# An S5 scan and a dilated local attention on one core: a memset moved to GpSimd, V's weight loads put on the Activation queue, and a new written-out order

## The chip, the cores and the metric

The kernel runs on one core of one Trainium2 chip. The metric is device time in microseconds of one execution. Before the change the median of three runs is 137.35 us (137.34 to 138.31).

## The reference, cut to what matters

Two independent layers read two inputs of 2048 rows and 448 columns in bf16, and their outputs stand side by side in the 896 columns of the result.

```python
# A: a diagonal complex state space layer
Bu = einsum("bld,pd->blp", x, B_bar)
h  = Lam_bar * h + Bu[:, t]                 # over 2048 steps
y  = 2 * einsum("blp,dp->bld", hseq, C).real + x * Dskip
# B: attention over 8 keys, 2 rows apart, 16 heads of 28
q, k, v = split(x @ wqkv)
attn = softmax(q . k[t - 2w] * scale, masked where t < 2w)
out  = (sum_w attn * v[t - 2w]) @ wo
```

## The kernel before, in words

The sequence of B is split into two halves of 1024 rows (index `b`). Weights and `x` are laid out so that the contraction runs over 128 rows: channel blocks are kept once for even and once for odd positions, so the weight matrix for Q and K (`wqk`, part of the tile `rb`) is loaded once and then copied to the other half of the partitions by `shift` (copies at L205 on DVE or L201 on ACT). The copies come in three column blocks: "a" (columns 0 to 127, loaded by L359 on the ACT queue), "b" (128 to 255) and "c" (256 to 447), both loaded by L359 on the SP queue. Each block has a copy of 64x6 and one of 64x8 rows; the second also needs the last 64 weight rows, loaded by L361 on the ACT queue. V's weights are a tile of their own (`wv`, `load_v`, lines L336 to L340 of `wload`): the even copy of 336 KB and 56 KB, and the odd copy of the same sizes, four transfers.

`x` for B arrives by transposing transfers: the first half in four pieces (`half(h, m)`, L348: `h` the quarter of the sequence, `m` the pair of positions), the second half in four pieces (`load(1, j)`, L352). For A, `x` arrives in 16 such transfers (L865, tile `xaT_sb`), and the matrices B by L845 and L846.

Projections of Q and K go first: for the first half `first(kt, h)` (L492) makes a pair of column blocks for 512 rows, with `h = 0` needing the first two pieces of `x` and `h = 1` the other two; block "c" and the leftover columns, and the whole second half, are made by `proj` (L451). Products of Q with shifted K are formed on DVE (L557, 18 instructions of 128x2048 or 128x4096), summed per head on PE with 32-column weights (L570), then softmax (L597, L606, L616 on ACT; L591, L625 on DVE). V's projection (L670) is spread to neighbours by transfers on SP (L696), DVE multiplies and adds (L724 to L741), transfers transpose the result (L768) and PE applies `wo` (L787, L794).

A's scan runs for seven groups `m` of 64 complex states: input projection (L1132), powers of Lambda as small matrices (`pw`, built by L1081 on DVE or as ten scaled copies on ACT), a tree of carries (L1149 to L1228) in which PE and ACT alternate, and the output product (L1316) with the skip term (L1335 on PE, or L1302 on DVE and L1328 on ACT).

The memsets and masks of `consts` and `consts2` stand ahead of everything else in the program: DVE clears tiles, GpSimd runs `affine_select` on them. In `consts2`, DVE clears the upper half of `Zhi` (L255) after GpSimd's second `affine_select` on it (L253).

All other work is cut into units, and each unit is added to a `Planner` with its engines, cost, latency and priority. The planner's result is written out: the list `ORDER` gives the units in program order (a number from 1000 up means the second of the unit's engines) and `BANKS` the PSUM banks. At build time `run` walks `ORDER`; costs and latencies no longer have any effect then. So each engine and each transfer queue executes its instructions in the order of that list, and waits by semaphores.

Transfers of the SP and ACT queues share eight semaphores (DMAHW0 to DMAHW7), handed out in turn in program order over both queues. A transfer waits, before its issue, for the landing of the transfer that had its semaphore before it, unless that is known to be done.

Of the kernel before, what the change touches and what calls it, by code (L numbers as in the profile page):

```python
# [9 lines left out]
ACT = mybir.ActivationFunctionType  # L10
# [6 lines left out]
D = 448  # L17
T = 16
# [11 lines left out]
JB = 8  # L30
SL = HALO + JB
NX = 7
KPAD = 16
# [41 lines left out]
]  # L75
BANKS = [
    0, 0, 2, 3, 5, 0, 2, 4, 6, 0, 2, 4, 6, 0, 6, 4, 0, 6, 4, 6, 0, 2, 4, 6, 7, 2, 0, 6, 7, 0, 7, 2, 0, 1, 2, 4,
    5, 2, 4, 5, 7, 2, 5, 2, 5, 3, 0, 2, 0, 5, 4, 7, 5, 0, 3, 2, 5, 0, 5, 0, 1, 6, 4, 6, 4, 6, 2, 0, 2, 0, 6, 4,
    2, 0, 2, 4, 6, 2,
# [112 lines left out]
class Ctx:  # L192
# [43 lines left out]
    def consts2(self):  # L236
        nc, pool, G, V = self.nc, self.pool, self.nc.gpsimd, self.nc.vector
# [17 lines left out]
        V.memset(Zh[0:64, :], 0.0)  # L255
# [56 lines left out]
class PartB:  # L312
# [9 lines left out]
    def loads(self):  # L322
# [24 lines left out]
        def half(h, m):  # L347
            nc.sync.dma_start(xh[:, 14 * m:14 * m + 14, 64 * h:64 * h + 64],  # L348
                              bass.AP(x.tensor, x.offset + 64 * h * JB * D + 4 * m * D, [[JB * D, 64], [1, 4 * D]]), transpose=True)
# [7 lines left out]
        def cols(eng, c0, c1):  # L357
            for a in range(2):
                eng.dma_start(w4[:, 0:3, a, c0:c1], src[:, :, a, c0:c1])  # L359
# [3 lines left out]
        self.u_w["a", 0] = P.add("ACTQ", 0.0, lambda: None, lat=5.6)  # L363
        self.u_wr = P.add("ACTQ", 0.0, lambda: None, lat=6.2)
        self.u_xh = {}
        for h in range(2):
            for m in range(2):
                self.u_xh[h, m] = P.add("SP", 1.33, lambda h=h, m=m: half(h, m), [self.u0], -9, lat=3.6 if h + m == 0 else 3.4, dma=1.04)
            c0, c1 = ((NCH, 2 * NCH), (2 * NCH, D))[h]
            self.u_w["bc"[h], 0] = P.add("SP", 0.95, lambda c0=c0, c1=c1: cols(nc.sync, c0, c1), [self.u0], -9, lat=3.4, dma=(0.9, 1.3)[h])  # L370
# [20 lines left out]
    def load_v(self, deps):  # L391
        def go():
            self.wload(self.nc.sync, 2 * D, 0)
            self.wload(self.nc.sync, 2 * D, 1)
        self.u_w[2] = self.plan.add("SP", 2.3, go, deps, 0.5, lat=1.6, dma=3.6)
# [30 lines left out]
    def prep(self, u_warm):  # L426
        nc, P, cx = self.nc, self.plan, self.cx
# [97 lines left out]
        for b in range(2):  # L525
            for n, (kind, kt) in enumerate((("K", 0), ("Q", 0), ("K", 1), ("Q", 1), ("K", 2), ("Q", 2), ("M", 3))):
                if b or kt > 1:
                    proj(b, kind, kt, -8 + b * 4 + 0.1 * n)

            def dup(b=b):  # L530
                t0, t1 = b * HB, (b + 1) * HB
                nc.sync.dma_start(self.k3[hi, KPAD + JB + t0:KPAD + JB + t1], self.k3[lo, KPAD + t0:KPAD + t1])
                nc.sync.dma_start(self.q3[hi, t0:t1], self.q3[lo, t0:t1])
            self.u_k[b, 3] = self.u_q[b, 3] = [P.add("SP", 1.0, dup, self.u_k[b, 3] + self.u_q[b, 3], -7, lat=1.5, dma=1.2)]
# [287 lines left out]
class PartA:  # L822
# [27 lines left out]
    def load_x(self, deps):  # L850
# [23 lines left out]
        for j in (0, 4, 8, 12, 2, 6, 10, 14, 1, 5, 9, 13, 3, 7, 11, 15):  # L874
            self.u_x[j] = P.add("SP", 1.36 if j < T - 1 else 1.9, lambda j=j: load(j), deps if j < T - 1 else [u0], 0.6, lat=1.6, dma=0.48)
# [22 lines left out]
    def setup(self):  # L898
# [132 lines left out]
        a4 = P.add("DVE", 1.9, u4, [a3], -5)  # L1031
# [443 lines left out]
```

## Time and profile before

| what | value |
|---|---|
| median of 3 runs | 137.35 us |
| the profiled execution's own time | 137.41 us |
| its span, first to last instruction | 135.7 us |
| outside the span | 1.7 us |
| PE, DVE, ACT, POOL busy | 126.7, 113.8, 99.1, 10.3 us |
| granted TensorE clock | 1.00 throughout |
| transfers | 20.25 MB, mean 149 GB/s |

PE is the tensor engine's matmuls and PEld its weight loads, DVE the vector engine, ACT the scalar engine, POOL GpSimd, SP the engine that issues most transfers; a q behind a name means its queue or sequencer. A row of the timeline gives the start in us from the span's start, the duration, the engine and line, what is written and read, the number of instructions merged into the row, and in brackets the idle time of the engine before it with what ended that. The chain of waits has start, duration and what ran. In a table by windows each engine has its busy time and number of instructions, then the granted clock, the mean busy share of the 16 DMA engines and the GB/s. The view of one source line ends with the time from a transfer's issue to its landing. In the DMA view q1 is the SP queue and q10 the ACT queue, with packets, MB and share of 16 engines. Busy PE is not PE at its peak: a 128x512 matmul is shown with some 380 ns, while the next one starts 216 ns later.

### The profile page before, as it was taken

To read this page: it belongs to the slowest core of one execution; us is meant where nothing else is said; L and a number is where in the kernel's file an instruction comes from. 1 tells how busy PE (TensorE), PEld (TensorE's weight loads), DVE (VectorE), ACT (ScalarE), POOL (GpSimd) and SP (SyncE) were. 2 spreads that over 40 slices of the span, in tenths; PEclk is the share of its full clock that TensorE was granted. 3 is DMA by queue.
4 is the path that set the end of the run, shared out by engine and by line. 5 is a ranking of instruction groups with operands and counts; after the bars stand their busy time and mean duration, and the time that the engine had idled before them with its cause. 6 is when DMAs were issued, how large, how long until landed. Compare 5 with 4: busy or idle time off the path is not lost.

```text
span 135.7 us, 2467 instructions
## 1 busy us (share of the span) xinstructions
PE 126.7 (93%) x921; PEld 63.5 (47%) x921; DVE 113.8 (84%) x133; ACT 99.1 (73%) x170; POOL 10.3 (8%) x27
## 2 busy tenths in 40 slices
PE   6859999999999689999999999999899999999990
PEld 2447543344446243565444455444556554455440
DVE  5069999999999996799999999999999999990100
ACT  3018999769797535798879997988889993527741
POOL 6934060000000000000000000000000000000000
PEclk9999999999999999999999999999999999999999
DMA  4999899589446586924669999261810394128432
GB/s 102 206 208 180 146 234 186 115 197 132 77 75 131 122 232 187 235 69 101 178 169 145 225 238 233 78 175 28 236 39 0 78 279 153 68 96 214 169 135 101
DMA packets 47759, 20.25 MB, mean 149 GB/s; under 512 B 38774, under 2 KB 46346, under 8 KB 47748
## 3 DMA queue, kind: packets, MB, share of 16 engines
q1 hardware_dynamic: 46676, 19.77, 62.8%
q10 hardware_dynamic: 880, 0.31, 1.1%
q8 instruction: 7, 0.11, 0.4%
q0 software_dynamic: 192, 0.03, 0.1%
q14 instruction: 4, 0.03, 0.1%
HBM read 5.18 MB, written 4.19 MB: 69 GB/s over the span
## 4 chain that ended last, share of the span: by engine, by line
PE 86%; ACT 4%; POOL 4%; issue 3%; DVE 1%; POOLq 0%; DVEq 0%; ACTq 0%
PE banks L1316 16%; PE banks L1132 15%; PE banks L451 12%; PE banks L670 8%; PE banks L787 7%; PE banks L570 6%; PE banks L492 5%; PE banks L1176 4%; PE banks L794 2%; PE banks L1149 2%; POOL prm L836 2%; PE banks L1189 1%; PE banks L1335 1%; PE banks L1056 1%; PE banks L1228 1%
## 5 line engine op out<-in xcount | busy, mean ns | idle before, releaser
L557 DVE TENSOR_TENSOR prods<-qk 128x4096 bf16<-128x4096 bf16 (+1 forms) x18 | 31.8, 1809 | 0.0
L1132 PE MATMUL banks<-xaT_sb,Bcat 128*128 128x512 bf16 (+1 forms) x112 | 27.0, 383 | 1.5 <-issue 1.5
L201 ACT CAST ra<-banks 128x896 bf16<-128x896 f32 (+2 forms) x24 | 18.5, 777 | 12.6 <-PE banks L1316 5.7
L201 ACT CAST qk<-banks 128x512 bf16<-128x512 f32 (+3 forms) x20 | 16.8, 844 | 2.4 <-PE banks L451 1.3
L730 DVE TENSOR_TENSOR prods<-prods 128x7168 bf16<-128x7168 bf16 x4 | 15.6, 3889 | 0.1
L724 DVE TENSOR_TENSOR prods<-ra 128x7168 bf16<-128x7168 bf16 x4 | 15.5, 3882 | 0.0
L724 DVE TENSOR_TENSOR prods<-ra,qk 128x7168 bf16<-128x7168 bf16 x4 | 15.4, 3883 | 0.0
L1132 PEld LDWEIGHTS <-Bcat 128*128 128x128 bf16 (+1 forms) x112 | 8.8, 99 | 12.9 <-issue 6.9
L1316 PE MATMUL banks<-Ccat,h 128*128 128x448 bf16 x64 | 14.7, 353 | 0.0
L451 PE MATMUL banks<-rb 128*128 128x512 bf16 (+1 forms) x64 | 13.9, 379 | 0.0
L670 PE MATMUL banks<-wv,rb 128*128 128x448 bf16 (+1 forms) x64 | 13.0, 354 | 0.0
L1171 ACT CAST pbuf<-banks 128x64 bf16<-128x64 f32 (+1 forms) x42 | 9.6, 233 | 3.4 <-PE banks L1176 2.2
L1316 PE MATMUL banks<-Ccat,qk 128*128 128x448 bf16 x48 | 12.0, 353 | 0.0
L787 PE MATMUL banks<-wo_p,rb 128*128 128x448 bf16 x48 | 11.1, 356 | 0.0
L1176 PE MATMUL banks<-pbuf,pw 128*128 128x64 bf16 x77 | 9.8, 235 | 0.6 <-ACT pbuf L1171 0.5
L492 PE MATMUL banks<-rb 128*128 128x256 bf16 (+2 forms) x76 | 7.3, 256 | 2.0 <-DVE rb L205 1.5
L203 ACT ACTIVATE qk<-banks 128x512 bf16<-128x512 f32 (+2 forms) x10 | 8.4, 848 | 0.8 <-PE banks L451 0.8
L1176 PEld LDWEIGHTS <-pw 128*128 128x128 bf16 x77 | 6.2, 105 | 5.5 <-issue 1.6
L1081 DVE TENSOR_TENSOR pw<-Dm,spair 128x640 bf16<-128x640 bf16 (+1 forms) x14 | 8.5, 649 | 0.0
L1316 PEld LDWEIGHTS <-h 128*128 128x128 bf16 x64 | 5.9, 98 | 5.3 <-issue 0.6
L451 PEld LDWEIGHTS <-rb 128*128 128x128 bf16 (+1 forms) x64 | 5.1, 97 | 6.7 <-issue 1.7
L670 PEld LDWEIGHTS <-rb 128*128 128x128 bf16 (+1 forms) x64 | 4.9, 98 | 6.2 <-issue 3.0
(144 smaller groups left out, 187.5 us busy)
## 6 DMA issues: line engine op xcount, KB each, us to landing
out_dram<-ra SPq DMA_DIRECT2D x12, 224.0 KB, 2.6
xaT_sb<-in_A_x_dram SPq DMA_DIRECT2D x2, 448.0 KB
out_dram<-ra SPq DMA_DIRECT2D x8, 112.0 KB, 1.7
ra<-ra SPq DMA_DIRECT2D x2, 392.0 KB, 3.8
qk<-qk SPq DMA_DIRECT2D x2, 392.0 KB, 3.8
wv<-in_B_wqkv_dram SPq DMA_DIRECT2D x2, 336.0 KB, 3.9
ra<-ra SPq DMA_DIRECT2D x1, 588.0 KB, 5.6
qk<-qk SPq DMA_DIRECT2D x1, 588.0 KB, 4.7
```

The lines of the kernel that those rows point to most:

```text
L201: nc.scalar.copy(out, in_)
L451: nc.tensor.matmul(out(e)[:, j0:j1], lhsT=w, rhs=self.xB[rows, b, j0:j1, c, :], start=e not in begun, stop=True, skip_group_check=True)
L492: nc.tensor.matmul(box["ps"][:, e, k, 64 * j0:64 * j1], lhsT=self.wqk[rows, c, D * k + NCH * kt:D * k + NCH * kt + NCH], rhs=self.xB[rows, ...
L557: V.tensor_tensor(p[:, :, a:a + n], q[:, t0 + a:t0 + a + n].unsqueeze(1).to_broadcast([NCH, 4, n]), bass.AP(k.tensor, k.offset, [k.ap[0], ...
L670: nc.tensor.matmul(box["ps"][:, e, 0:D], lhsT=self.xB[rows, b, jj, c, :], rhs=self.wv[rows, c, :], start=e not in begun, stop=True, skip_g ...
L724: V.tensor_tensor(out.rearrange("p (u i d h) -> p u i d h", u=4, i=4, d=DH), self.attn[b][:, r].rearrange("p (x u i) h -> p x u i h", x=2, ...
L730: V.tensor_tensor(T1, T1, T2, op=ALU.add)
L787: nc.tensor.matmul(ps, lhsT=o[:, kt + x, :], rhs=self.wo_p[:, (KT + 1) * x + kt, :], start=(kt == 0), stop=False, skip_group_check=True)
L1132: mt(ps(i), lhsT=lhsT, rhs=rhs, start=i not in begun, stop=True, **kw)
L1171: nc.scalar.copy(pb[:, dst, PAD:PAD + NCH // d], tot(a, d))
L1176: mt(tot(out, 2), lhsT=L(T * unit * k), rhs=pb[:, src, PAD - sh:PAD - sh + NCH // 2], start=False, stop=True, **kw)
L1316: nc.tensor.matmul(ps, lhsT=self.h[m][:, i, g * NCH:(g + 1) * NCH], rhs=self.Ccat[:, m, :], start=False, stop=(m == NM - 1), skip_group_ch ...
```

## The change

- In `consts2` the memset of `Zhi`'s upper half is on GpSimd, not DVE.
- `load_v` and the row copies `dup` (L532, L533) may be issued by SP or ACT. In the new list V's weights are on ACT (unit 134 is `1134`); both row copies are on SP, as before.
- Landing latencies and some costs given to the planner are changed, among them 2.5 us instead of 1.6 for A's `x`.
- `ORDER` and `BANKS` are new lists. Among the units that can go either way, two of the first-column `pw` builds (276 and 375) and one weight copy (17) are now on ACT, and two output evictions (590 and 595) on DVE.

```diff
 ORDER = [
-    3, 0, 1, 23, 4, 15, 2, 5, 6, 7, 9, 39, 41, 43, 16, 47, 8, 44, 45, 24, 46, 18, 25, 27, 40, 42, 59, 57, 17,
...
+    0, 1, 23, 3, 2, 5, 6, 15, 7, 8, 9, 10, 4, 41, 39, 16, 40, 44, 46, 42, 47, 43, 13, 24, 45, 57, 59, 11, 14,
+    12, 21, 1134, 1017, 18, 58, 60, 25, 61, 54, 53, 51, 27, 52, 50, 28, 22, 29, 20, 48, 49, 65, 149, 64, 67, 62,
...
-        V.memset(Zh[0:64, :], 0.0)
+        G.memset(Zh[0:64, :], 0.0)
...
-        self.u_w["a", 0] = P.add("ACTQ", 0.0, lambda: None, lat=5.6)
-        self.u_wr = P.add("ACTQ", 0.0, lambda: None, lat=6.2)
+        self.u_w["a", 0] = P.add("ACTQ", 0.0, lambda: None, lat=4.8)
+        self.u_wr = P.add("ACTQ", 0.0, lambda: None, lat=5.7)
...
-        def go():
-            self.wload(self.nc.sync, 2 * D, 0)
-            self.wload(self.nc.sync, 2 * D, 1)
-        self.u_w[2] = self.plan.add("SP", 2.3, go, deps, 0.5, lat=1.6, dma=3.6)
+        def go(eng):
+            q = self.nc.sync if eng == "SP" else self.nc.scalar
+            self.wload(q, 2 * D, 0)
+            self.wload(q, 2 * D, 1)
+        self.u_w[2] = self.plan.add(("SP", "ACT"), (2.3, 2.1), go, deps, 0.5, lat=1.9, dma=3.6)
...
-            def dup(b=b):
+            def dup(eng, b=b):
...
-            self.u_k[b, 3] = self.u_q[b, 3] = [P.add("SP", 1.0, dup, self.u_k[b, 3] + self.u_q[b, 3], -7, lat=1.5, dma=1.2)]
+            self.u_k[b, 3] = self.u_q[b, 3] = [P.add(("SP", "ACT"), (1.1, 1.05), dup, self.u_k[b, 3] + self.u_q[b, 3], -7, lat=2.0, dma=1.2)]
```

Three places show what moved. The first is DVE at the end of the opening memsets, before (`Zhi`, `mrow` and `mcol` are constants, `rb` holds the weights):

```order
L250 MEMSET Zhi 128x16 [waits DVE_49]
L255 MEMSET Zhi 64x24 [waits Pool_49]
L259 MEMSET mrow 128x56
L262 MEMSET mcol 128x64
L263 MEMSET mcol 128x16 [waits DVE_49]
L205 COPY rb<-rb 64x6x128 [waits DMAHW2_49,DMAHW0_49]
```

and with the change:

```order
L250 MEMSET Zhi 128x16 [waits DVE_49]
L259 MEMSET mrow 128x56
L262 MEMSET mcol 128x64
L263 MEMSET mcol 128x16 [waits DVE_49]
L205 COPY rb<-rb 64x6x128 [waits DMAHW2_49,DMAHW0_49]
L205 COPY rb<-rb 64x8x128 [waits DMAHW4_49]
```

DVE no longer waits for GpSimd ahead of the weight copies; the copies wait for landings alone.

The second is ACT from the program's start, with the change; before, the four `wv` rows and the copy `rb<-rb` behind them are not there, and L931 (now L933) follows the table load:

```order
L359 DMA rb<-in_B_wqkv_dram 128x3x128 x2
L361 DMA rb<-in_B_wqkv_dram 64x896
L362 ACT_TABLE_LOAD
L339 DMA wv<-in_B_wqkv_dram 128x3x448 [waits DMAHW0_49]
L340 DMA wv<-in_B_wqkv_dram 64x448 [waits DMAHW2_49]
L336 DMA wv<-in_B_wqkv_dram 128x3x448 [waits DMAHW4_49]
L337 DMA wv<-in_B_wqkv_dram 64x448 [waits DMAHW6_49]
L201 COPY rb<-rb 64x6x128 [waits DMAHW5_49]
L933 ACTIVATE dt_bf<-pf 128x7 [waits DVE_49]
L201 CAST qk<-banks 128x512 [waits PE_49]
```

V's weights come from the middle of SP's list to the front of ACT's, and each of the four waits for an earlier transfer: the last for the second transfer of block "b".

The third is SP at the start, before (L348 and L352 are B's `x`, L359 blocks "b" and "c"):

```order
L348 DMA_TRANSPOSE rb<-in_B_x_dram 128x14x64
L348 DMA_TRANSPOSE rb<-in_B_x_dram 128x14x64 [waits DMAHW0_49]
L359 DMA rb<-in_B_wqkv_dram 128x3x192 [waits DMAHW1_49]
L359 DMA rb<-in_B_wqkv_dram 128x3x192 [waits DMAHW2_49]
L352 DMA_TRANSPOSE rb<-in_B_x_dram 128x7x128 [waits DMAHW3_49]
L352 DMA_TRANSPOSE rb<-in_B_x_dram 128x7x128 [waits DMAHW4_49]
```

and with the change:

```order
L348 DMA_TRANSPOSE rb<-in_B_x_dram 128x14x64
L348 DMA_TRANSPOSE rb<-in_B_x_dram 128x14x64 [waits DMAHW1_49]
L359 DMA rb<-in_B_wqkv_dram 128x3x192 [waits DMAHW3_49]
L359 DMA rb<-in_B_wqkv_dram 128x3x192 [waits DMAHW5_49]
L352 DMA_TRANSPOSE rb<-in_B_x_dram 128x7x128 [waits DMAHW7_49]
L352 DMA_TRANSPOSE rb<-in_B_x_dram 128x7x128 [waits DMAHW0_49]
```

With V's four taking four of the eight semaphores, the first L352 now waits for DMAHW7, which belongs to the third L348 in the list, where it waited for the second.

More of the change, by code (lines that the diff above doesn't have):

```diff
@@ L46 @@
 ORDER = [
[28 rows of a table removed]
[28 rows of a table added]
 ]
 BANKS = [
-    0, 0, 2, 3, 5, 0, 2, 4, 6, 0, 2, 4, 6, 0, 6, 4, 0, 6, 4, 6, 0, 2, 4, 6, 7, 2, 0, 6, 7, 0, 7, 2, 0, 1, 2, 4,
-    5, 2, 4, 5, 7, 2, 5, 2, 5, 3, 0, 2, 0, 5, 4, 7, 5, 0, 3, 2, 5, 0, 5, 0, 1, 6, 4, 6, 4, 6, 2, 0, 2, 0, 6, 4,
-    2, 0, 2, 4, 6, 2,
+    0, 0, 2, 3, 5, 0, 2, 4, 6, 2, 4, 0, 6, 4, 2, 0, 2, 4, 0, 2, 4, 0, 4, 6, 7, 0, 2, 6, 0, 7, 6, 2, 0, 1, 2, 4,
+    5, 2, 5, 4, 7, 5, 2, 2, 5, 3, 2, 0, 0, 6, 5, 4, 6, 0, 3, 2, 6, 0, 6, 0, 1, 6, 4, 6, 4, 2, 6, 2, 0, 2, 6, 0,
+    4, 2, 6, 0, 4, 2,
 ]
@@ L367, in loads @@
             for m in range(2):
-                self.u_xh[h, m] = P.add("SP", 1.33, lambda h=h, m=m: half(h, m), [self.u0], -9, lat=3.6 if h + m == 0 else 3.4, dma=1.04)
+                self.u_xh[h, m] = P.add("SP", 1.33, lambda h=h, m=m: half(h, m), [self.u0], -9, lat=(3.3, 3.0, 3.2, 2.9)[2 * h + m], dma=1.0)
             c0, c1 = ((NCH, 2 * NCH), (2 * NCH, D))[h]
-            self.u_w["bc"[h], 0] = P.add("SP", 0.95, lambda c0=c0, c1=c1: cols(nc.sync, c0, c1), [self.u0], -9, lat=3.4, dma=(0.9, 1.3)[h])
+            self.u_w["bc"[h], 0] = P.add("SP", 0.95, lambda c0=c0, c1=c1: cols(nc.sync, c0, c1), [self.u0], -9, lat=(3.4, 3.0)[h], dma=(0.9, 1.2)[h])
         for j in range(4):
@@ L528, in prep @@
                     proj(b, kind, kt, -8 + b * 4 + 0.1 * n)
-            def dup(b=b):
+            def dup(eng, b=b):
                 t0, t1 = b * HB, (b + 1) * HB
-                nc.sync.dma_start(self.k3[hi, KPAD + JB + t0:KPAD + JB + t1], self.k3[lo, KPAD + t0:KPAD + t1])
-                nc.sync.dma_start(self.q3[hi, t0:t1], self.q3[lo, t0:t1])
-            self.u_k[b, 3] = self.u_q[b, 3] = [P.add("SP", 1.0, dup, self.u_k[b, 3] + self.u_q[b, 3], -7, lat=1.5, dma=1.2)]
+                q = nc.sync if eng == "SP" else nc.scalar
+                q.dma_start(self.k3[hi, KPAD + JB + t0:KPAD + JB + t1], self.k3[lo, KPAD + t0:KPAD + t1])
+                q.dma_start(self.q3[hi, t0:t1], self.q3[lo, t0:t1])
+            self.u_k[b, 3] = self.u_q[b, 3] = [P.add(("SP", "ACT"), (1.1, 1.05), dup, self.u_k[b, 3] + self.u_q[b, 3], -7, lat=2.0, dma=1.2)]
     def qk(self, b, prio):
@@ L874, in load_x @@
         for j in (0, 4, 8, 12, 2, 6, 10, 14, 1, 5, 9, 13, 3, 7, 11, 15):
-            self.u_x[j] = P.add("SP", 1.36 if j < T - 1 else 1.9, lambda j=j: load(j), deps if j < T - 1 else [u0], 0.6, lat=1.6, dma=0.48)
+            self.u_x[j] = P.add("SP", 1.36 if j < T - 1 else 1.9, lambda j=j: load(j), deps if j < T - 1 else [u0], 0.6, lat=2.5, dma=0.5)
         self.u_xx = {i: self.cx.double(512, self.xT[PL:NCH, i:T:4, 3, :], self.xT[0:PL, i:T:4, 3, :],
@@ L1030, in setup @@
         a3 = P.add("ACT", 0.22, u3, [a2], -5)
-        a4 = P.add("DVE", 1.9, u4, [a3], -5)
+        a4 = P.add("DVE", 2.4, u4, [a3], -5)
         a4b = P.add("POOL", 0.8, u4b, [a2, cx.boot], -4.5, lat=0.2)
```

53 rows, old and new, of the table ORDER are left out of this document.

## The prediction

> **What bounds the kernel now.** I read the table by windows first: whatever keeps PE from working moves the end.
>
> ```profile
> 0.00:5.00 5.00, 3.68 (x11) 1.41 (x12) 1.80 (x37) 1.28 (x1) 3.58 (x11) 1.00 0.69 137
> 5.00:10.00 5.00, 3.00 (x34) 2.04 (x33) 2.06 (x10) 0.32 (x2) 2.60 (x10) 1.00 1.11 207
> 10.00:46.00 36.00, 36.00 (x314) 17.77 (x314) 35.45 (x43) 30.72 (x41) 4.11 (x8) 1.00 0.76 146
> 45.00:50.00 5.00, 3.49 (x35) 1.35 (x24) 5.00 (x4) 1.42 (x3) 0.00 (x0) 1.00 0.72 176
> 60.00:100.00 40.00, 39.20 (x264) 19.38 (x263) 39.79 (x20) 35.08 (x78) 0.00 (x0) 1.00 0.66 156
> 130.00:135.70 5.70, 2.34 (x13) 0.80 (x10) 0.00 (x0) 1.48 (x3) 0.00 (x0) 1.00 0.35 120
> ```
>
> The first number after each length is PE's. PE is never idle from 10 to 46. Its 9.0 us of idle time (135.7 less 126.7 busy) lie at the start (1.32 and 2.00), around 47 (1.51), in the small waits of A's carries (0.80 between 60 and 100) and at the end (3.36, the last eviction and its transfer, which the change leaves). DVE is nearly as full, 35.45 of 36 and 39.79 of 40. So a gain is a PE gap that closes and stays closed. The timeline shows the first gap, and the views of two source lines show which landings stand around it.
>
> ```profile
> 6.29 0.54 PE L492 MATMUL banks<-rb 128*128 128x128 bf16 x4 [0.53 <-DMA rb<-in_B_x_dram]
> ...
> 7.05 0.08 DVE L255 MEMSET Zhi<- 64x24 uint32 x1 [3.93 <-POOL Zhi L253]
> 7.44 1.14 DVE L205 COPY rb<-rb 64x768 bf16<-64x768 bf16 x3
> 8.30 0.83 PE L492 MATMUL banks<-rb 64*128 64x256 bf16 x9 [1.47 <-DVE rb L205]
> 11.09 0.55 PEld L492 LDWEIGHTS <-rb 64*128 64x128 bf16 x12 [0.21 <-issue]
> ```
>
> ```profile
> L361 ACTq DMA_DIRECT2D rb<-in_B_wqkv_dram x1: 529/529/529, 1.8 to 1.8; - x1
> ...
> DMA to landing us min/median/max: 3.7/3.7/3.7
> ```
>
> ```profile
> L348 SPq DMA_TRANSPOSE rb<-in_B_x_dram x1: 1256/1256/1256, 4.7 to 4.7; - x1
> ...
> DMA to landing us min/median/max: 4.4/4.4/4.4
> ```
>
> ```profile
> L348 SPq DMA_TRANSPOSE rb<-in_B_x_dram x1: 1305/1305/1305, 6.0 to 6.0; - x1
> ...
> DMA to landing us min/median/max: 3.7/3.7/3.7
> ```
>
> DVE stands at the memset L255 for 3.93 us because GpSimd is late, and behind it in DVE's queue are the weight copies L205. Their last source landed at 1.8 + 3.7 = 5.5, but they start at 7.44, and PE waits for them until 8.30. The other gap is around 47:
>
> ```profile
> 47.89 0.39 PE L1132 MATMUL banks<-xaT_sb,Bcat 64*128 64x512 bf16 x2 [1.51 <-issue]
> ```
>
> ```profile
> L865 SPq DMA_TRANSPOSE xaT_sb<-in_A_x_dram x1: 1295/1295/1295, 43.3 to 43.3; - x1
> ...
> DMA to landing us min/median/max: 4.5/4.5/4.5
> ```
>
> ```profile
> L865 SPq DMA_TRANSPOSE xaT_sb<-in_A_x_dram x15: 1257/1267/2187, 13.7 to 43.3; - x15
> ...
> DMA to landing us min/median/max: 2.7/3.8/5.4
> ```
>
> No releaser is named ("issue"), but 43.3 + 4.5 = 47.8: PE waits for the last transfer of A's `x`, which in SP's order comes right behind the row copies of the second half and took 4.5 us where the fastest of its kind took 2.7.
>
> **The memset on GpSimd.** The wait and the 0.08 us leave DVE; the copies can start at 5.5. PE, which also needs the piece that landed by 6.29, resumes at about 6.3 to 6.8 instead of 8.30. On GpSimd the memset costs nothing that counts: POOL works 10.3 us in all, and its first results after the opening (the masks of the softmax) are used after 30. But the start cannot gain these 1.5 to 2.0 us. The matmuls of the second quarter need two pieces that landed at 4.7 + 4.4 = 9.1 and 6.0 + 3.7 = 9.7, and PE reached them at 11.09. It can come at most 11.09 - 9.7 = 1.4 us earlier, if these landings stay.
>
> **V's weights ahead of the first `x`.** They do not stay. V's four transfers now issue right behind ACT's table load.
>
> ```profile
> 2.37 1.28 ACT L362 ACT_TABLE_LOAD   x1 [2.37 <-issue]
> ...
> 26.32 0.58 SPq L339 DMA_DIRECT2D wv<-in_B_wqkv_dram  x1
> ```
>
> ```profile
> DMA packets 850, 0.26 MB, mean 260 GB/s; under 512 B 811, under 2 KB 850, under 8 KB 850
> ...
> q10 hardware_dynamic: 439, 0.17, 92.3%
> q1 hardware_dynamic: 380, 0.09, 42.3%
> ```
>
> ```profile
> q1 hardware_dynamic: 795, 0.19, 93.2%
> ```
>
> The first of the two DMA answers is the window from 3 to 4, where both queues have work: together they move 0.26 MB in the microsecond, and SP's queue gets 0.09. The second is 5 to 6, where SP's queue is alone: 0.19. Until the last piece lands at 9.7 SP's queue has about 0.19 x 4.8 = 0.91 MB from 4.9 on (my estimate of when V's bytes begin to move: between 3.65, where the table load ends, and 5.5, where ACT's last earlier transfer has landed). V's weights add 0.784 MB. At 0.26 MB/us the 1.70 MB last 6.5 us, so the piece lands at 4.9 + 6.5 = 11.4 and PE waits some 0.3 us longer than before. The start term is **-0.3**. Bounds: +1.4 if V's packets delay nothing, and 9.7 + 0.784/0.26 = 12.7, that is -1.6, if V's whole 3.0 us come out of the pieces of `x`. I take the middle value because both mixed and single rates are in the rows.
>
> A rule of the Trainium skill speaks against the move (DMA: Bandwidth & Descriptors, section Issuing engines are not separate DMA queues): transfers issued by several engines run on the same 16 DMA engines and interleave, and a second issuer saves only the time to issue. The 0.09 against 0.19 MB of SP's queue agree. By it the start term would be -1.6 at worst; without it +1.4.
>
> The semaphores matter on SP as well. The first L352 now waits for the third L348, about 9.1 before and some 10.5 with the contention, instead of issuing at 8.5.
>
> ```profile
> L352 SPq DMA_TRANSPOSE rb<-in_B_x_dram x4: 1220/1296/1296, 8.5 to 12.4; - x4
> ...
> DMA to landing us min/median/max: 3.8/3.8/3.8
> ```
>
> ```profile
> 18.16 2.75 PE L451 MATMUL banks<-rb 128*128 128x512 bf16 x12
> ```
>
> SP's list is then 2.0 us late. The last of the four landed at 12.4 + 3.8 = 16.2, now 18.2 or a little more; PE starts on the second half of the sequence inside the row at 18.16, after six matmuls of 0.22, at 19.5. It fits with 1 us to spare, so this costs 0. On ACT, the fourth V transfer waits until the second transfer of block "b" has landed (about 7.3), and the copy and the step size's exponential behind it on ACT wait with it. Before, ACT was idle to past 9:
>
> ```profile
> 9.51 0.21 ACT L931 ACTIVATE dt_bf<-pf 128x7 bf16<-128x7 f32 x1 [5.85 <-DVE pf L927]
> ```
>
> The copy's 0.8 us after 7.3 ends ahead of that, so this is 0 too; it costs what the wait passes 8.7 by.
>
> **The gap at 47.** V's four issues, 4 x 0.58 = 2.3 us, leave SP, and with the 2.0 us of the late start the last transfer of A's `x` is issued 0.3 us earlier, or 0.7 if the start is less late: at some 42.6. In the new order three other transfers of A's `x` stand between it and the row copies of the second half, where before it followed them directly; at 2.7 us it lands at 45.3. PE, which arrives at 46.4 before and at about 45.1 with what it gains, then waits 0.2 us or so instead of 1.51. I take **+1.2**; bounds 0 (it lands in contention again) and +1.5.
>
> **Switches on PE.** PE loses time when it goes from full matmuls to 64-row or 32-column ones, as the chain of waits shows:
>
> ```profile
> 22.32 3.45 PE banks L451 x18
> ...
> 33.06 0.65 PE banks L451 x3
> ```
>
> Three full matmuls take 0.65 us, 0.216 each. The 18 are 12 full ones and six of 64 rows that run in pairs: 15 x 0.216 = 3.24, and 0.21 are left for two switches. I count 59 switches in the old order and 55 in the new: 4 x 0.10 = **+0.4**, bounds 0 and 0.4. The new order of the carries may close or open the 0.80 us between 60 and 100: value 0, bounds -0.8 and +0.8, since no row tells the new order's waits.
>
> **More work on ACT.** Two `pw` builds of ten copies each and one weight copy go from DVE to ACT.
>
> ```profile
> L1171 ACT CAST pbuf<-banks 128x64 bf16<-128x64 f32 x35 | 7.7, 224 | 2.5 <-PE banks L1176 1.4 <-PE banks L1166 0.3
> ```
>
> ```profile
> 12.64 1.15 ACT L201 COPY rb<-rb 64x1152 bf16<-64x1152 bf16 x1
> ```
>
> The nearest row for one scaled copy is 224 ns, so 20 take about 4.6 us with some margin; the weight copy, 768 of 1152 elements, 0.8. In all 5.4 us, between 10 and 46, where ACT has 36 - 30.72 = 5.28 us idle. It is only just hidden, if the idle pieces lie where the work stands. Value 0; if the cover is gone, the second rival below. The row copies stay on SP, so that edit by itself does nothing.
>
> **Sum.** -0.3 + 1.2 + 0.4 = 1.3 us gained; 137.41 - 1.3 = **136.1**. The profiled execution's 137.41 is 0.06 above the median, so no correction. The bounds give 1.6 + 0.8 = 2.4 lost (139.8) and 1.4 + 1.5 + 0.4 + 0.8 = 4.1 gained (133.3).
>
> **Rivals.** First, V's weights fill holes and slow nothing (for it: SP's queue alone moves 0.19 where both move 0.26; against it: 0.09 between 3 and 4). Then 1.4 + 1.5 + 0.4 = 3.3. A limit comes from DVE, whose last results are transposed for the last products of B:
>
> ```profile
> L768 SPq DMA_TRANSPOSE rb<-rb x1: 1255/1255/1255, 121.2 to 121.2; - x1
> ...
> DMA to landing us min/median/max: 2.6/2.6/2.6
> ```
>
> ```profile
> 126.45 1.30 PE L787 MATMUL banks<-wo_p,rb 128*128 128x448 bf16 x6
> ```
>
> They land at 123.8, 2.65 us ahead of PE. If DVE does not come earlier itself, PE can gain 2.65; if it does, 3.3. I put this rival at 134.5.
>
> Second, the slower side: ACT becomes the bound of the stage from 10 to 46.
>
> ```profile
> 37.10 1.02 ACT L606 ACTIVATE ex_sb<-banks 128x1024 bf16<-128x1024 f32 x1 [0.75 <-PE banks L601]
> ```
>
> Of the 5.28 us idle much is ACT waiting for PE, as here; if half of it cannot be filled, 5.4 - 2.6 = 2.8 us are left over, evictions come late by that much, and PE waits for banks. Time: 137.41 + 2.8 - 1.3 = 138.9. It decides from the point at which the first exponential starts after about 39.5 instead of 37.10. Against it: DVE gets the freed time, and evictions can stand ahead of the builds in the list.
>
> Third, no net change: all 3.0 us of V's bytes come out of the first pieces of `x`. -1.6 + 1.2 + 0.4 = 0, 137.4. It is what the two-queue window would say if ACT's larger packets keep two thirds of the rate (0.17 of 0.26) throughout. The rule of the Trainium skill named above allows this case.
>
> **How the numbers follow.** A measurement of this kernel tells about 1% from no change, that is below 136.0 or above 138.7. The forecast has 0.46, its own range 135.4 to 137.0 (0.20 of it below 136.0, 0.26 above); V's weights for free 0.22, faster; ACT as the bound 0.16, slower; no net change 0.16. That gives faster 0.20 + 0.22 = 0.42, same 0.26 + 0.16 = 0.42, slower 0.16. The range of 8 in 10 takes in the first and the third rival and ends where the second begins: 134.2 to 138.7.
>
> **What would show it.** Right: no wait for POOL on DVE, the copies at about 5.5, PE back at 6.3 to 6.8; the fourth piece of `x` landing near 11.4 and PE waiting there; the first L352 near 10.5; the PE gap around 45 to 47 under 0.5 us. Wrong: a landing near 9.7 (first rival) or 12.7 and later (third); an exponential after 39.5, and PE rows that wait for ACT between 10 and 46 (second); a gap at 47 that stays, because the last transfer still lands 4 us after its issue.

## The result, and the profile after

The changed kernel takes 136.56 us (median of 20 runs, 135.54 to 139.06) against 137.3 (20 runs, 136.67 to 138.54); the ratio is 0.9923, with a 95% interval of 0.9897 to 0.9948. The profiled execution took 136.07, with a span of 134.4 us where before it was 135.7. The forecast was 136.1, in a range of 134.2 to 138.7. A second measurement gave a median of 137.5 (12 runs) and a ratio of 0.9993, 0.9958 to 1.0028; it is told with the experiments. The ratio 0.9923 leaves out seven of the change's 20 executions, which took over 1.5% longer than its fastest; the two medians by themselves give 0.9946. The two measurements do not agree; together they leave anything from no gain to 1%.

The table by windows of the changed kernel (columns as before):

```profile
0.00:5.00 5.00, 3.68 (x9) 1.34 (x10) 2.37 (x41) 1.28 (x1) 3.56 (x11) 1.00 0.68 132
5.00:10.00 5.00, 3.90 (x38) 2.29 (x36) 1.03 (x3) 0.83 (x1) 2.95 (x12) 1.00 1.22 273
10.00:46.00 36.00, 35.35 (x303) 17.05 (x304) 34.02 (x42) 34.28 (x56) 3.17 (x7) 1.00 0.80 145
45.00:50.00 5.00, 5.00 (x34) 2.19 (x27) 5.00 (x4) 4.72 (x14) 0.00 (x0) 1.00 0.69 167
60.00:100.00 40.00, 39.02 (x258) 19.21 (x255) 39.79 (x19) 35.24 (x74) 0.00 (x0) 1.00 0.64 152
130.00:134.40 4.40, 1.01 (x6) 0.29 (x3) 0.35 (x1) 0.53 (x1) 0.00 (x0) 1.00 0.46 156
```

PE's idle time fell from 9.0 to 7.5 us (134.4 less 126.9 busy). Against before: the start, 0 to 46, is 0.25 better (1.32 + 1.10 + 0.65 for 1.32 + 2.00), the gap at 47 is gone (1.51), the carries are 0.18 worse and the tail 0.03. The gap, then, is the gain, and the start gave next to nothing although the wait for GpSimd is gone. The timeline of the start shows why:

```profile
5.68 0.42 DVE L205 COPY rb<-rb 64x1024 bf16<-64x1024 bf16 x1 [0.76 <-DMA rb<-in_B_wqkv_dram]
...
8.65 0.47 ACTq L337 DMA_DIRECT2D wv<-in_B_wqkv_dram  x1
...
8.68 0.83 PE L493 MATMUL banks<-rb 128*128 128x256 bf16 x6 [0.50 <-DMA rb<-in_B_wqkv_dram]
...
9.17 0.83 ACT L201 COPY rb<-rb 64x768 bf16<-64x768 bf16 x1 [5.51 <-DMA wv<-in_B_wqkv_dram]
...
10.05 1.15 PE L493 MATMUL banks<-rb 128*128 128x256 bf16 x10 [0.55 <-ACT rb L201]
...
10.41 5.25 SPq L352 DMA_TRANSPOSE rb<-in_B_x_dram  x4
...
11.81 3.12 PE L493 MATMUL banks<-rb 64*128 64x256 bf16 x28 [0.60 <-DMA rb<-in_B_x_dram]
```

```profile
L348 SPq DMA_TRANSPOSE rb<-in_B_x_dram x1: 1302/1302/1302, 4.7 to 4.7; - x1
...
DMA to landing us min/median/max: 5.7/5.7/5.7
```

DVE copies as soon as the weights land (5.68). But the third piece of `x` now takes 5.7 us instead of 4.4 and the fourth lands just before 11.81, where it was 9.7; V's last issue waits on ACT until 8.65, and the copy behind it ends at 10.0. PE waits three times: 0.50 us for block "b" itself (8.68), 0.55 for the copy (10.05) and 0.60 for the fourth piece (11.81).

### The profile page after: what moved, and what is told of

Read it like the earlier page. It is cut to its first block, busy times and chain, and to the rows that moved or that the text cites. A ratio compares the mean times of both kernels' runs of the same rounds, so it can differ in the third digit from the quotient of the medians.

```text
span 134.4 us, 2479 instructions
## 1 busy us (share of the span) xinstructions
PE 126.9 (94%) x921; PEld 63.5 (47%) x921; DVE 113.8 (85%) x131; ACT 103.4 (77%) x189; POOL 9.7 (7%) x28
## 4 chain that ended last, share of the span: by engine, by line
PE 82%; ACT 6%; DMA 4%; SPq 4%; issue 1%; ACTq 0%
PE banks L1318 15%; PE banks L1134 15%; PE banks L452 12%; PE banks L672 8%; PE banks L789 7%; PE banks L572 6%; DMA rb<-in_B_x_dram 4%; PE banks L1178 3%; SPq L348 3%; PE banks L493 2%; PE banks L1151 2%; PE banks L796 2%; PE banks L1191 2%; ACT eP L1147 1%; ACT pbuf L1173 1%
## 5 line engine op out<-in xcount | busy, mean ns | idle before, releaser
L201 ACT CAST ra<-banks 128x896 bf16<-128x896 f32 (+2 forms) x22 | 16.9, 802 | 8.6 <-PE banks L1318 5.2
L1134 PEld LDWEIGHTS <-Bcat 128*128 128x128 bf16 (+1 forms) x112 | 9.0, 100 | 10.5 <-issue 4.0
L789 PE MATMUL banks<-wo_p,rb 128*128 128x448 bf16 x48 | 10.5, 354 | 0.0
L493 PE MATMUL banks<-rb 128*128 128x256 bf16 (+2 forms) x76 | 7.9, 256 | 1.8 <-DMA rb<-in_B_x_dram 0.6
L452 PEld LDWEIGHTS <-rb 128*128 128x128 bf16 (+1 forms) x64 | 5.0, 97 | 7.1 <-issue 2.5
L1147 ACT CAST eP<-banks 128x1024 bf16<-128x1024 f32 x7 | 7.2, 1023 | 1.5 <-PE banks L1134 1.5
L201 ACT CAST h<-banks 128x512 bf16<-128x512 f32 (+1 forms) x8 | 6.5, 808 | 1.9 <-PE banks L1191 1.8
```

Of the source, the lines that this page charges most:

```text
L201: nc.scalar.copy(out, in_)
L452: nc.tensor.matmul(out(e)[:, j0:j1], lhsT=w, rhs=self.xB[rows, b, j0:j1, c, :], start=e not in begun, stop=True, skip_group_check=True)
L493: nc.tensor.matmul(box["ps"][:, e, k, 64 * j0:64 * j1], lhsT=self.wqk[rows, c, D * k + NCH * kt:D * k + NCH * kt + NCH], rhs=self.xB[rows, ...
L789: nc.tensor.matmul(ps, lhsT=o[:, kt + x, :], rhs=self.wo_p[:, (KT + 1) * x + kt, :], start=(kt == 0), stop=False, skip_group_check=True)
L1134: mt(ps(i), lhsT=lhsT, rhs=rhs, start=i not in begun, stop=True, **kw)
```

## The experiments

**The memset alone.** Before, with one line changed:

```diff
-        V.memset(Zh[0:64, :], 0.0)
+        G.memset(Zh[0:64, :], 0.0)
```

> Before with one line changed: the memset of Zhi's upper half on GpSimd, order and V's loads as before. Theory (the landing of A's last x, which SP's list sets, is what PE meets at 47): PE resumes at some 6.3 instead of 8.30 and reaches the work around 46 about 1.4 us earlier, but that transfer is still issued at 43.3 and lands at 47.8, so the gap there grows from 1.51 to 2.9 us and the time stays: 137.3 (ratio 0.998 to 1.002). Rival (a gain at the start carries to the end): 137.3 - 1.4 = 135.9, ratio 0.990.

Measured: 137.09 us, ratio 0.9975 (0.9943 to 1.0006). The time stays within the noise, but not by the wait that I named. The timeline of this run:

```profile
18.54 0.39 PE L451 MATMUL banks<-rb 64*128 64x512 bf16 x2 [2.18 <-DMA rb<-in_B_x_dram]
```

```profile
45.00:50.00 5.00, 5.00 (x51) 2.38 (x50) 5.00 (x5) 3.09 (x4) 0.00 (x0) 1.00 0.64 156
```

PE comes early to the second half of the sequence and waits 2.18 us for its `x`. It then comes to the last transfer of A's `x` at 47.57, and that one landed 2.6 us after its issue, at 46.66, so the gap there is gone. What PE gains at the start it loses at the landing of the second half.

**The gap alone.** Before, with A's last transfer (unit 125) ahead of the row copies (114):

```diff
-    ..., 130, 127, ..., 114, 189, ..., 144, 212, 208, 133, 125, 284, ...
+    ..., 130, 127, ..., 125, 114, 189, ..., 144, 212, 208, 133, 284, ...
```

> Before with one unit moved in the order: the last transfer of A's x is issued ahead of the second half's row copies instead of right behind them; everything else as before. Theory: it is issued at about 42.05 and lands uncontended at about 44.8, PE does not wait at 46.4, the gap of 1.51 us goes and 135.9 us is left (ratio 0.989). Rival (the row copies, now 1.3 us later, hold DVE's products and hand the wait on): 137.0 to 137.4.

Measured: 137.22, ratio 0.9992 (0.9968 to 1.0016). The rival is right. On DVE and on PE (the profile is of the longest of the 12 executions, 137.8):

```profile
48.89 4.49 DVE L557 TENSOR_TENSOR prods<-qk 128x4096 bf16<-128x4096 bf16 x2 [1.66 <-PE banks L670]
```

```profile
53.43 0.61 PE L570 MATMUL banks<-prods,Zsel 128*32 128x512 bf16 x8 [0.68 <-DVE prods L557]
```

The page names PE for DVE's wait, but these products read the row copies, which SP issued at 44.4 and 45.1 in this run. The second of them:

```profile
L533 SPq DMA_DIRECT2D qk<-qk x1: 541/541/541, 45.1 to 45.1; - x1
...
DMA to landing us min/median/max: 3.7/3.7/3.7
```

It landed at 48.8, just ahead of DVE's start at 48.89, so it is what DVE waited for. SP issues one transfer after the other up to 45 us, and whichever of the two comes last is waited for.

**V's weights early, alone.** Before, with `load_v` as in the change and unit 134 as `1134` ahead of ACT's first activation:

```diff
-    ..., 27, 40, ..., 136, 134, 137, ...
+    ..., 1134, 27, 40, ..., 136, 137, ...
```

> Before with V's four weight transfers at the front of ACT's list, directly behind the table load; the memset stays on DVE, the order is otherwise as before. Theory: V's bytes delay the fourth piece of B's x from 9.7 to 11.4 to 11.8, so PE loses 0.3 to 0.7 at the start; SP loses the 2.3 us of V's issues and gets about 2.0 back from the later first L352, so A's last x, still right behind the row copies, is issued near 43.0 and lands near 47.5: the gap at 47 shrinks by as much as PE comes later, 137.0 to 137.3 in all. Rival (taking V off SP's queue is what brings the gain): A's last x comes 2 us earlier and 136.0 or less.

Measured: 138.7, ratio 1.0085 (1.0051 to 1.0119): worse than either theory. PE in this run:

```profile
12.60 3.34 PE L493 MATMUL banks<-rb 64*128 64x256 bf16 x32 [1.10 <-DMA rb<-in_B_x_dram]
19.79 0.39 PE L452 MATMUL banks<-rb 64*128 64x512 bf16 x2 [1.16 <-DMA rb<-in_B_x_dram]
```

The first wait is the fourth piece (some 0.8 later than I had allowed), the second the second half, which the later first L352 pushes back. Together with the memset, in the old order (`load_v` again as in the change):

```diff
-        V.memset(Zh[0:64, :], 0.0)
+        G.memset(Zh[0:64, :], 0.0)
-    ..., 27, 40, ..., 136, 134, 137, ...
+    ..., 1134, 27, 40, ..., 136, 137, ...
```

> Before with the memset on GpSimd and V's weights at the front of ACT's list, but the old order for all else. Theory (the parts alone bring nothing; the new order, with three transfers between the row copies and A's last x, is needed): V's cost of 0.85% less what the memset gives back: 137.2 to 137.8, ratio 0.999 to 1.003. Rival (the two parts are the change, the order beside them is noise): 136.3, ratio 0.992.

Measured: 139.08, ratio 1.0105 (1.0073 to 1.0136). Neither theory; the two parts in the old order cost 1%. Its timeline and its windows (the third column from the end is the granted clock) show something that I had not reckoned with:

```profile
7.15 1.09 PE L493 MATMUL banks<-rb 128*128 128x128 bf16 x13 [0.73 <-DMA rb<-in_B_x_dram]
10.27 1.15 PE L493 MATMUL banks<-rb 128*128 128x256 bf16 x10 [0.63 <-DVE rb L205]
12.62 4.95 PE L493 MATMUL banks<-rb 64*128 64x256 bf16 x32 [1.21 <-DMA rb<-in_B_x_dram]
```

```profile
12.00:14.00 2.00, 1.38 (x11) 0.76 (x11) 1.94 (x4) 1.19 (x3) 0.32 (x1) 0.66 0.93 208
14.00:16.00 2.00, 2.00 (x11) 1.45 (x10) 1.97 (x3) 0.51 (x1) 0.00 (x0) 0.50 1.07 161
16.00:18.00 2.00, 2.00 (x17) 1.53 (x16) 0.60 (x2) 1.47 (x3) 0.00 (x0) 0.98 1.16 151
```

The clock falls to half here. It is only a part of the loss: two of the six executions have a mean clock of 1.00, where the others have 0.988, and still took 138.3 and 138.4.

**The memset back on DVE**, all else as in the change:

```diff
-        G.memset(Zh[0:64, :], 0.0)
+        V.memset(Zh[0:64, :], 0.0)
```

> The changed kernel with the memset of Zhi's upper half back on DVE; everything else as in the change. Theory: PE again resumes at 8.3, but the fourth piece of B's x lands at about 11.7 anyway and the work of the first two quarters fits before it; the time stays within 0.3 us of the change: 136.4 to 136.8. Rival (the memset is what brings the change's gain): 1.4 us later, 137.9.

Measured: 137.37, ratio 1.0004 (0.9977 to 1.0032). Beside the change's first measurement that is 0.8% lost, beside its second nothing. What the memset is worth within the change is between these, and stays open in the times. In the profile it is next to nothing: PE again waits for DVE's copies, to 8.32, but then only 0.28 us for the fourth piece, and its waits in the first 20 us without the opening matmuls (counted as in the account below) are 2.7 us, beside 2.9 and 2.6 in the two profiles of the change. That is the theory's mechanism.

**V's weights on SP again**, behind the second half of B's `x`:

```diff
-    12, 21, 1134, 1017, ...
+    12, 134, 21, 1017, ...
```

> The changed kernel with V's four weight transfers on SP again, right behind the second half of B's x (four L352) instead of at the front of ACT's list. Theory (what frees the start runs into the next landing): the fourth piece of B's x lands near 9.8 instead of 11.7 and PE comes up to 2 us earlier, but the four L352, issued from 8.5, land only at 17.5 to 18.5 and PE waits for them at about 16 to 18; A's last x is issued near 42.8 and lands near 45.5 without a long gap. 136.0 to 136.6, ratio 0.990 to 0.995. Rival (V's bytes beside the first x cost the change its start gain): 2 us less than the change, 134.3 to 134.8.

Measured: 136.82, ratio 0.9968 (0.9943 to 0.9994); a little behind the theory's 0.990 to 0.995 and far from the rival. The start is as expected: the 21 matmuls of the second half begin at 18.02 instead of 19.73, and no wait for `x` is left ahead of them, so the wait at 16 to 18 that I expected was wrong. The 1.7 us are given back by the row copies, which SP issues 0.8 us later still, at 26.45:

```profile
29.90 4.49 DVE L559 TENSOR_TENSOR prods<-qk 128x4096 bf16<-128x4096 bf16 x2 [2.33 <-DMA qk<-qk]
```

```profile
18.02 4.16 PE L452 MATMUL banks<-rb 128*128 128x512 bf16 x21
...
32.25 0.62 PE L572 MATMUL banks<-prods,Zsel 128*32 128x512 bf16 x8 [0.97 <-DVE prods L559]
...
34.45 0.62 PE L572 MATMUL banks<-prods,Zsel 128*32 128x512 bf16 x8 [0.72 <-DVE prods L559]
...
46.59 1.41 PE L1134 MATMUL banks<-xaT_sb,Bcat 64*128 64x512 bf16 x5 [0.47 <-issue]
```

The last row is the place of the gap at 47: with V's issues on SP, 0.47 of the 1.51 us are left there.

**Three other places for V's weights.** Later on ACT, behind its first four evictions:

```diff
-    12, 21, 1134, 1017, ..., 63, 1019, ...
+    12, 21, 1017, ..., 63, 1134, 1019, ...
```

> The changed kernel with V's four transfers later on ACT, behind the first four evictions (at about 11 to 12 us). Theory: the fourth piece of B's x lands near 9.8, but V's 3 us of bytes now run beside the second half of B's x, which lands 1 to 3 us later than 18, and ACT's evictions behind V's issues come 2 us later: 136.5 to 138. Rival (only the first four pieces are sensitive): 134.3 to 135.0.

Measured: 147.65, ratio 1.0755 (1.0717 to 1.0793). Neither: ACT's next copy shows it.

```profile
21.94 0.47 ACTq L337 DMA_DIRECT2D wv<-in_B_wqkv_dram  x1
22.46 1.15 ACT L201 COPY rb<-rb 64x1152 bf16<-64x1152 bf16 x1 [11.36 <-DMA ra<-in_A_B_re_dram]
```

V's fourth issue shares its semaphore with a transfer of A's matrices, which SP issued at 14.93 and which landed at 21.92, and ACT stood behind it for 11.36 us. Then right behind the weight copy, from 7.85 to 11.9:

```diff
-    12, 21, 1134, 1017, ...
+    12, 21, 1017, 1134, ...
```

> The changed kernel with V's four transfers on ACT behind the weight copy (at about 9 us) instead of ahead of it. Theory: the fourth piece of B's x lands near 9.8 to 10.3, but four issues of 0.4 to 0.5 us hold the first evictions on ACT, so that DVE's first product is 1 to 2 us later than it could be and half of the start's gain goes: 135.4 to 136.4. Rival (an issue on ACT waits for a late SP transfer through a shared semaphore, as in the run with V behind the first evictions): 138 or more.

Measured: 137.47, ratio 1.0027 (0.9999 to 1.0054), between the two; the mechanism is the rival's. The fourth issue waited again (to 11.45), the first eviction came at 12.08, and PE waited for it:

```profile
13.20 1.47 PE L493 MATMUL banks<-rb 128*128 128x256 bf16 x12 [1.60 <-ACT qk L203]
```

Last by GpSimd, at 9.6 to 12.4 (a 2000 in the order is a unit's third engine, which the unit is given):

```diff
-            q = self.nc.sync if eng == "SP" else self.nc.scalar
+            q = {"SP": self.nc.sync, "ACT": self.nc.scalar, "POOL": self.nc.gpsimd}[eng]
-    12, 21, 1134, 1017, ..., 29, ...
+    12, 21, 1017, ..., 29, 2134, ...
```

> The changed kernel with V's four transfers issued by GpSimd at about 10.5 us, in its idle time, through semaphores that SP and ACT do not share; the rest as in the change. Theory (V's bytes beside the first pieces of x cost the change its start, V's issues on SP would cost it the row copies, and neither is needed): the fourth piece of B's x lands near 9.8, PE is about 1.7 us ahead of the change at 15, V's bytes fall beside the second half of B's x, which delays it by up to 1.5 us, and SP's row copies come 2 us earlier than in the change: 134.6 to 135.6, ratio 0.981 to 0.988. Rival (there is no free place for V's bytes before 20; the second half of x comes as late as V costs it): 136.2 to 136.8.

Measured: 140.56, ratio 1.0212 (1.0173 to 1.0252); both theories too low. PE, and its windows:

```profile
20.96 5.28 PE L452 MATMUL banks<-rb 128*128 128x512 bf16 x12 [3.09 <-ACT qk L203]
```

```profile
18.00:20.00 2.00, 0.00 (x0) 0.00 (x0) 2.00 (x4) 1.95 (x4) 0.00 (x0) 1.00 1.10 63
20.00:24.00 4.00, 3.04 (x8) 1.11 (x9) 2.55 (x3) 2.11 (x2) 0.00 (x0) 0.50 1.17 234
```

These are the matmuls that began at 18.02 in the run with V's weights on SP, where the same eviction ended at 21.15 and held nothing. So it is not ACT that they wait for, but most likely the second half of `x`. SP's queue was still moving small packets, of which `x` is made, from 19 to 20:

```profile
DMA packets 260, 0.07 MB, mean 67 GB/s; under 512 B 260, under 2 KB 260, under 8 KB 260
```

The last small packets ahead of A's matrices ended at 16.7 in the run with V's weights on SP and at 20.2 here. V's last transfer landed at 19.94, so the two were on their way together; why `x` moved only 0.07 MB in that microsecond stays open. The granted clock is 1.00 to 20 and 0.50 from there on, in the middle of the wait.

**The `pw` builds back on DVE**, all else as in the change:

```diff
-    ..., 95, 1375, 155, ..., 310, 1276, 208, ...
+    ..., 95, 375, 155, ..., 310, 276, 208, ...
```

> The changed kernel with the two pw builds (units 375 and 276) on DVE again; everything else as in the change. Theory: ACT's 4.6 us were hidden in its idle time and DVE's two times 0.48 us are hidden in the 2.65 us by which its last results come ahead of PE: within 0.3 us of the change, 136.0 to 136.8. Rival (ACT holds the stage from 10 to 46): 135.5 or less. Other rival (DVE holds it): 137.2.

Measured: 143.54, ratio 1.0428 (1.038 to 1.0477). All three were wrong. At these places of the list DVE has products of 2.2 us each ahead of the build, and the carries' first matmul waits:

```profile
53.99 0.63 PE L1151 MATMUL banks<-eP,pw 128*128 128x512 bf16 x1 [4.77 <-DVE pw L1083]
```

```profile
50.00:54.00 4.00, 0.01 (x1) 0.14 (x3) 4.00 (x5) 0.00 (x0) 0.00 (x0) 0.66 0.60 195
54.00:58.00 4.00, 4.00 (x10) 1.13 (x9) 1.00 (x2) 0.59 (x1) 0.00 (x0) 0.50 0.78 210
```

The gap at 47 is gone in this run too (PE's matmuls at 46.30 wait for nothing); the builds on ACT keep the next step from waiting. A build is 0.48 us on DVE, but its queue is 5 us behind. (Earlier in DVE's list it would be another case, not tried.)

**The change again**, with nothing edited:

> The changed kernel again, to stand beside the other two on the same chip: 136.0 to 136.6, ratio 0.990 to 0.995 under every theory.

Measured: 137.5 (136.24 to 138.74), ratio 0.9993 (0.9958 to 1.0028): outside what I expected. Its profile was taken of the fastest execution and has the same waits as the first (0.54 us for ACT's copy, 0.64 for the fourth piece), so it does not show what the longer executions met.

**A version from these findings.** V's weights on SP behind the second half of `x`, and the row copies, which were late then, by GpSimd, which is idle:

```diff
-    12, 21, 1134, 1017, ..., 99, 84, ..., 187, 114, 169, ...
+    12, 134, 21, 1017, ..., 99, 2084, ..., 187, 2114, 169, ...
-                q = nc.sync if eng == "SP" else nc.scalar
+                q = {"SP": nc.sync, "ACT": nc.scalar, "POOL": nc.gpsimd}[eng]
```

> The changed kernel with V's four transfers on SP behind the second half of B's x (as in the run with V on SP) and the four row copies of both halves issued by GpSimd, which is idle then. Theory (SP's list, one issue after the other to 45 us, is the pace; each issue taken off it without early bytes counts): the first row copies go out when ACT's evictions end, near 23.5 instead of 26.45, and land near 28, so DVE's wait of 2.33 us falls to 1 or less, and A's last x is issued 2.4 us earlier and lands near 44, so that nothing waits at 46: 136.8 - 1.2 - 0.5 = 135.1, between 134.6 and 135.7, ratio 0.980 to 0.989. Rival (PE and DVE run into another wait, so that it all is given back as in the runs before): 136.4 to 137.2.

Measured: 135.56 (134.71 to 136.21), ratio 0.9875 (0.9833 to 0.9918), as the theory has it. All six executions are shorter than the 11 of before beside them (136.56 and up). The change was not run beside it; its medians were 136.56 and 137.5. Its windows, the copies on POOL and DVE, which no longer waits for them:

```profile
5.00:10.00 5.00, 4.57 (x51) 3.15 (x50) 2.37 (x10) 2.01 (x4) 3.35 (x13) 1.00 1.06 203
10.00:46.00 36.00, 35.09 (x296) 16.63 (x294) 34.50 (x38) 33.62 (x55) 5.20 (x9) 1.00 0.87 165
45.00:50.00 5.00, 5.00 (x31) 2.08 (x28) 5.00 (x3) 4.15 (x12) 0.00 (x0) 1.00 0.54 120
```

```profile
19.74 0.62 POOL L534 DMA_DIRECT2D qk<-qk  x1 [3.30 <-ACT qk L201]
...
32.20 0.56 POOL L534 DMA_DIRECT2D qk<-qk  x1 [9.05 <-ACT qk L201]
```

```profile
22.70 9.27 DVE L559 TENSOR_TENSOR prods<-qk 128x4096 bf16<-128x4096 bf16 x5
```

PE's idle time is 7.3 us (133.8 less 126.5); the largest wait left between the start and the tail is 0.91 us at 37.7, for a transfer of A's `x`. The row copies by GpSimd with V's weights left on ACT were not run, so what each of the two moves brings by itself is not shown.

## Why the prediction was right, and where it was not

**The size and the sign** held in the first measurement: 136.1 forecast, 136.07 in the profiled execution, 136.56 in the median. The second median, 137.5, lies in the range too, but there is no gain in it. By step, in the profiles:

- *The memset.* The last copy that the first matmuls need came at 5.68 (forecast about 5.5), and the start gained little because the fourth piece of `x` came later: right. The experiment with the memset alone shows no gain clear of the noise. (I had GpSimd's first results used after 30; its `den` is read by DVE near 18, but it began at 9.45, no later than the 9.56 before.)
- *V's weights, -0.3.* Mechanism and size held. I forecast the third piece at 10.5 (measured 4.7 + 5.7 = 10.4), the first L352 at 10.5 (10.41) and the fourth piece at 11.4 (PE got it at 11.81). Counted from the start of one matmul to the start of the next, less the time of its columns and without the switches, PE's waits in the first 20 us grew from 4.21 to 4.79. (By idle time the same stretch is 0.25 better; the page models the ends of matmuls, and the starts are measured.) Of these 0.58 us, 0.32 are not V's. They lie in the eleven opening matmuls, which the change leaves alone. Before:

```profile
1.32 4.04 PE L286 MATMUL banks<-prods 128*128 128x512 bf16 x11 [1.32 <-DVE prods L278]
```

with the change, and in the second profile of the same kernel:

```profile
1.32 4.42 PE L286 MATMUL banks<-prods 128*128 128x512 bf16 x11 [1.32 <-DVE prods L278]
```

```profile
1.32 4.87 PE L286 MATMUL banks<-prods 128*128 128x512 bf16 x11 [1.32 <-DVE prods L278]
```

They start 0.43 us apart at first and 0.22 apart later, from 4.3 us on before and from 5.1 on with the change; in the second profile all of them are 0.43 apart. This differs between two executions of one kernel, and the granted clock of 1.00 in the tables does not show it. The first projection follows at 5.26 before and at 5.58 after. What is left, 0.26, stands against the forecast's 0.3. The Trainium skill's rule that queues share the 16 engines (DMA: Bandwidth & Descriptors, section Issuing engines are not separate DMA queues) agrees with the 5.7 against 4.4 us. It does not give the size: of the 3.0 us of V's bytes about 2 came out of the pieces of `x`.

- *ACT behind V's fourth transfer, 0.* This step failed. I had the second transfer of block "b" land at 7.3, which no row shows. It landed at 8.63, and at 8.16 in the run with V's weights on SP, so most of the error is not V's doing. V's last issue came at 8.65 and took 0.47 us itself, which my bound of 8.7 left out; the copy ended at 10.0, and PE waited 0.50 for the block and 0.55 for the copy. It did not add to the end because the fourth piece was later still.
- *The four L352 "with 1 us to spare", 0.* Right in number, wrong in reasoning. The landing of the last of them was not in the trace; I had taken it from another's 3.8 us, and the place where PE first reads it from the order. The memset-alone run puts PE's wait for it at 16.4 to 18.5. The margin in the old order was near nothing, and in the new order the second half stands later on PE (19.73).
- *The gap at 47, +1.2.* The last transfer was issued at 42.4 (forecast 42.6) and PE did not wait at all: 1.51. The 0.2 us of waiting that I left there were an error of the sum: I let PE come 1.3 us earlier, at 45.1, but 1.2 of these are gained only at this gap. By the other terms it comes at about 46.3, behind the landing that I put at 45.3. The run with that transfer alone moved shows that this move by itself does not bring it, since the row copies are late in its place. With V's weights on SP and the new list, 0.47 us of the gap are left, and PE comes there 0.5 us later than in the change (46.1 for 45.6). So the new places of the copies and of A's `x` have a part in it and V's 2.3 us off SP another; how much each brings is not shown. The `pw` builds on ACT are not what closes it, but without them the next step waits 4.77 us.
- *Switches, +0.4.* 59 became 55; from start to start they fell from 5.98 to 5.57 us.
- *ACT's extra work, 0.* ACT went from 30.72 to 34.28 of 36 between 10 and 46, and the change held. The reason that I gave (DVE gets a little time) was too weak, as the run with the builds on DVE shows. My sign of ACT as the bound, a first exponential after 39.5, came true and meant nothing: the new list has other work of ACT ahead of it.

```profile
39.82 1.03 ACT L608 ACTIVATE ex_sb<-banks 128x1024 bf16<-128x1024 f32 x1
```

The sum as measured: -0.3 for the opening matmuls, which had no term, -0.3 + 1.5 + 0.4 = 1.3, the 1.3 us by which the spans differ, with the smaller terms near zero. That it meets the forecast's 1.3 so closely is luck: the gap gave 0.3 more than its term, and the opening happened to take as much away.

**What stays open** is why the second measurement of the change lies 0.7% above the first. There is one profile for each run, and none of a longer execution of the change. A lower clock is a part of it at most: in the second measurement the two longest executions, 138.34 and 138.74, have a mean clock of 1.00. Before, two late landings (at 18 and 47) meet PE at fixed times and may well swallow what varies at the start, and in the changed kernel nothing behind the start does so; that is argued, not shown.

## What to carry to other kernels

Where one queue issues without a pause, as SP's does here, look for the list of landings that PE meets, in order, before pricing a single wait. Here removing the first wait only moved PE to the next, and swapping two transfers on the same queue only changed which one was late. Take whole issues off that queue, and give them to an engine that is idle then and whose semaphores the busy queues do not share; and move bytes only to a time at which nothing that PE needs is in flight.

## What the runs showed of the hardware that was not expected

The clock fell by half, and not only after long waits. In the wait of 4.77 us above, which began at 49.2, the granted clock was 0.66 on average between 50 and 54 and 0.50 after it; if it only has the values 1 and 0.5, it fell near 51.3, 2.1 us into the wait. In the wait of 3.09, which began at 17.9, it fell at 20, again 2.1 us in. And in the run of both parts in the old order it fell to 0.66 and 0.50 from 12 on after three waits of 0.73, 0.63 and 1.21 us in 6.2 us, and was back at 0.98 from 16 on. The Trainium skill has the gate halve the clock after an idle window of some 3.4 us (TensorE: Matmul & The Clock Gate, section What's actually happening). None of the three cases fits that: the first two fell sooner, and the third has no idle window of that length at all. By the third, short waits close together count as well. My prices of the start's waits had no such cost. Nor is it rare: of the 23 executions of before beside the second measurement, six have a mean clock of 0.984 or 0.985, which is about 4 us of 136 at half the clock and more than the idle tail of 3.36, though the profile of before has no wait of PE over 1.51 us ahead of the tail.

An issue on ACT can hold ACT until a transfer of SP has landed: 11.36 us in the run above, by one of the eight shared semaphores.
